# Two buffers for ScalarE's half of a decoding scratch, and one each for two small copies, in an attention and expert kernel

## The chip, the cores and the metric

The kernel runs on one core of a Trainium2 chip. The metric is device time in microseconds (us) of one launch. The kernel before ran three times: 1174.45, 1170.73 and 1174.22 us, median 1174.22 us.

## The reference

Eight batches of eight heads, 576 positions, head dimension 64, go through linear attention with 128 random features, and the result goes through a gated layer of 512 x 1536. All in float32:

```
proj = x @ w_phi                       # x is q or k
proj = proj - max(abs(proj), last axis)
phi(x) = concat(exp(proj), exp(-proj)) # 256 features
kv  = phi(k)^T v ;  z = sum over positions of phi(k)
attn = (phi(q) kv) / (phi(q) z + 1e-6)
X = attn as 4608 tokens x 512
out = ((X @ w_a) * (X @ w_b)) @ w_out
```

The weights w_a, w_b and w_out arrive in 64-bit form and have to be decoded on the chip: of each number the high and the low 32-bit word are read, and two float32 halves are made of them that TensorE multiplies by one after the other ("hi" and "lo").

## The kernel before, in words

A *pair* is two heads of one batch; there are 32. For each pair the kernel projects q and k, forms the features, multiplies, and divides; a pair takes four *turns* of a plan that is written out by hand (`attention_steps`). Beside the attention runs the first pass of the gated layer over the first 6 of 12 slices of the 1536 columns (`moe_block`), and after both a second pass over the other slices, with Strassen-like sums (`winograd`, from about 800 us on).

The weights of the first pass, 18 *units* (6 slices of each of w_a, w_b, w_out), are decoded during the attention by `load_weights`, in four steps a unit. The plan lets 0.8 steps go per turn from turn 5 on and 2.2 per turn from turn 40 on. A unit's life, all on tiles of 128 x 512:

1. ScalarE (L427, `Prelu`) turns the high words of the raw tile into `g`. It is queued behind the last exponential of the latest projection. Right behind it ScalarE's queue issues the transfer of the next unit's raw tile (L402); there are two raw tiles.
2. VectorE (L430) shifts `g` into `s`; (L432) masks `g`.
3. ScalarE (L435) casts `s` to the high half that TensorE uses.
4. VectorE (L437) multiplies the low words into `g` (last reader of the raw tile), (L438) takes the high half from `s`, and (L440) adds `s` and `g` to the low half.

`g` and `s` are the two halves of one tile `w` of 128 x 1024. It has one buffer in pool `a1`; up to turn 28 the units take it in turn from `a1` and from the pool `early`, so that two are in use there.

Two more tiles matter. `dn` (L299, L300) is the copy of a pair's row sums that ScalarE takes out of PSUM; SyncE (SP) stores it to HBM (L312, `den`), loads it back in another shape (L315), VectorE takes the reciprocal (L317), and it goes out (L319, `rec`) and is read back spread over the partitions (L323, `rb`), to be multiplied in (L326). `rk` (L159) holds the last 64 positions of k for two pairs. Both have two buffers.

What sets the order: TensorE's products in the attention are chained in the order in which the program writes them. ScalarE, VectorE and SP take their instructions strictly in the order of their queues; that order is made at build time by a planner, which walks the program with its own costs and puts an instruction into its engine's queue when its inputs, and the buffer that it writes, are free by these costs. So a change of buffers can change the order of the queues. [...]

PSUM results of the projection go through `p` copies: L201 copies the first half of q's projection, L213 the second; TensorE can write the second half of a pair's q (`pq`) only when L201 has emptied its buffer.

Of the kernel before, what the change touches and what calls it, by code (L numbers as in the profile page):

```python
# [9 lines left out]
F32 = mybir.dt.float32  # L10
# [8 lines left out]
P = 128  # L19
# [25 lines left out]
def tile_kernel(ctx, tc, qP, km, kr, vm, vr, w_phi, eye, w_a, w_b, w_out, out):  # L45
# [17 lines left out]
    DM, NT = out.shape  # L63
    DF = w_a.shape[0]
    NFULL = S // P
    HALF = S // 2
# [37 lines left out]
    def mm(out, w, x, start=True, stop=True):  # L104
        issue = lambda: nc.tensor.matmul(out, w, x, start=start, stop=stop, skip_group_check=True)  # L105
        return pe(issue) if alone else issue()
# [8 lines left out]
    def bank(tag, name):  # L115
        if "ps" in alone:
            return alone["ps"].tile([P, 3, P], F32, tag=tag, name=name)
        if tag == "kv":
            return alone["att"].tile([P, 3, P], F32, tag="kv", bufs=1, name=name)
        if tag == "pt":  # L120
            return alone["att"].tile([P, 2, 512], F32, tag="att", name=name)[:, 0, : 3 * P].rearrange("p (s f) -> p s f", s=3)
        return pools_moe[0].tile([P, 3, P], F32, tag="moe", name=name)
# [29 lines left out]
    def load_kq(b, pr, a1, a2, consts, st):  # L152
        u = f"{b}_{pr}"
        k32 = a2.tile([P, NFULL * P], F32, tag="k32", name=f"k32_{u}")
        loads.append(nc.sync.dma_start(k32, km[b, pr]))
        q32 = a2.tile([P, S], F32, tag="q32", name=f"q32_{u}")
        loads.append(nc.sync.dma_start(q32, qP[b, pr]))
        if pr % 2 == 0:
            rk = a2.tile([P, P], F32, tag="rk", name=f"rk_{u}")  # L159
            loads.append(nc.sync.dma_start(rk, kr[b, pr // 2]))  # L160
            st["rk", b, pr // 2] = rk
        st["k", b, pr], st["q", b, pr] = k32, q32
# [128 lines left out]
    def den_products(b, pr, a1, a2, consts, st):  # L291
        u = f"{b}_{pr}"
        kvh, eq = st["kvh", b, pr], st["eq", b, pr]
        pd = bank("pt" if "ps" in alone else "pd", f"pd_{u}").rearrange("p s f -> p (s f)")
        for s in range(2):
            for j in range(2):
                for t in range(2):
                    mm(pd[strips[2 * j + t], :HALF], kvh[:, 2, strips[2 * j + s]], eq[:, j, s, times[t]], start=(s == 0), stop=(s == 1))
        dn = st["dn", b, pr] = a2.tile([P, HALF], F32, tag="dn", name=f"dn_{u}")  # L299
        nc.scalar.activation(dn, pd[:, :HALF], AF.Identity, bias=consts[3])  # L300

    def behind(what, issue):
# [28 lines left out]
    def attention_steps(pools, consts, st):  # L331
# [11 lines left out]
        for i in range(B * NPAIR):  # L343
            b, pr = divmod(i, NPAIR)
            t0 = TURNS * i
            args = (b, pr, *pools, consts, st)
            at = SPREAD if i < ALONE else PACKED
            if i == ALONE - 1:
                at = dict(SPREAD, turned_kv=8, num_products=8, den_products=8)
            elif i == ALONE:  # L350
                at = dict(PACKED, kv_products=4, z_products=4, kv_out=4)
            units = ((project, 0), (q_features, TURNS), (turned_kv, 0), (summed, 0), (kv_products, 0), (num_products, 0), (z_products, 0), (kv_out, 0))
            units += ((den_products, 0), (load_kq, -5), (load_v, -2 if i else 0))
            for order, (f, t) in enumerate(units):
                if f is not summed or i >= SUM_FROM:
                    plan(order, once(f, *args), [t0 + at.get(f.__name__, t)])
            rec_turns = REC_TURNS0 if b < B - 1 else REC_TURNS
            done = t0 + at["den_products"]
            plan(10, reciprocals(b, pr, *pools, st), [done + t for t in rec_turns])
            if b == 0:  # L360
                plan(11, x_first, [done + rec_turns[-1] + t for t in X_TURNS])
            if pr == NPAIR - 1:
                plan(12, b, [done + rec_turns[-1]])
# [41 lines left out]
    def raw_tiles(units, stage):  # L405

        for f, nm in units:
            yield load_raw(0, f, nm, stage)

    def load_weights(units, a1):  # L410

        def stage(kind, shape, dt, name):
            return a1.tile(shape, dt, tag="raw", bufs=2, name=name)

        tiles = raw_tiles(units, stage)
        raws = deque([next(tiles)])
        yield
        for f, nm in units:
            raw = raws.popleft()
            u = f"0_{f}_{nm}"  # L420
            low, high = raw[:, :, 0], raw[:, :, 1]
            place = alone["early"] if alone["turn"] < TURNS * ALONE - 8 and len(weights) % 2 else a1
            w = place.tile([P, 2 * DM], F32, tag="w", name=f"w_{u}")
            g, s = w[:, :DM], w[:, DM:]
            gb, sb = g.bitcast(U32), s.bitcast(U32)
            with tc.issue_after(acts[-1].ins):
                prelu = nc.scalar.activation(g, high.bitcast(F32), AF.Prelu, scale=2.0**-112, alpha=2.0**32)  # L427
            with tc.issue_after(prelu.ins):
                raws.extend(itertools.islice(tiles, 1))
            nc.vector.tensor_scalar(sb, gb, 3, None, op0=ALU.logical_shift_left)  # L430
            yield
            nc.vector.tensor_scalar(gb, sb, 0xFF800000, None, op0=ALU.bitwise_and)  # L432
            t = wpool.tile([P, 2, DM], F32R, tag=f"w_{f}_{nm}", name=f"w_{u}")
            hi, lo = t[:, 0], t[:, 1]
            nc.scalar.copy(hi, s)  # L435
            yield
            nc.vector.scalar_tensor_tensor(g, low, 2.0**-52, g, op0=ALU.mult, op1=ALU.mult)  # L437
            nc.vector.tensor_tensor(s, s, hi, op=ALU.subtract)  # L438
            yield
            nc.vector.tensor_tensor(lo, s, g, op=ALU.add)  # L440
            weights[0, f, nm] = (hi, lo)
            yield
# [443 lines left out]
    with ExitStack() as c:  # L886
# [5 lines left out]
        work, tasks, due, coded, st = deque(), {}, 0.0, 0.0, {}  # L892
        units = [(f, nm) for f in range(NFS[0]) for nm in "ab"] + [(f, "o") for f in range(NFS[0])]
        decode_steps = placed(load_weights(units, pools[0]))
        for turn, ready in attention_steps(pools, consts, st):
            if ready is not None:
# [155 lines left out]
```

## Time and profile before

| | |
|---|---|
| three runs, median | 1174.22 us |
| the profiled execution | 1174.8 us |
| its span, first to last instruction | 1172.9 us |
| busy TensorE matmul / weight load | 97% / 88% |
| busy VectorE / ScalarE / GpSimd | 63% / 48% / 12% |
| mean granted TensorE clock | 0.994 |

The profile gives each instruction's start and duration in microseconds from the span's start, by engine: PE is TensorE, PEld its weight load, DVE VectorE, ACT ScalarE, SP SyncE; a q behind the name (SPq, ACTq) is the engine's queue, which issues transfers. Releasers of waits are inferred from semaphores. [...]

### The profile page before, as it was taken

Reading aid. Unit: us, or ns where it says so; the run is one execution under the profiler, and the core shown is the slowest. Engines: PE = TensorE matmul, PEld = TensorE weight load, DVE = VectorE, ACT = ScalarE, POOL = GpSimd, SP = SyncE. Lnnn points to the kernel's source line nnn. Section 1 sums busy time; section 2 is a strip of 40 time slices with the busy share of each in tenths; the row PEclk is TensorE's granted clock in tenths of the full one; section 3 lists DMA queues with packets and bytes.
Section 4 is the critical chain, followed back from the end, with each engine's and each line's share of the span. In section 5 each row is a group of like instructions: output and inputs, shape, how many; then the busy total and the mean of one; then the engine's idle time right before and its main releaser. Section 6 shows DMA issues by size and latency. Waiting matters only on the chain.

```text
span 1172.9 us, 20997 instructions
## 1 busy us (share of the span) xinstructions
PE 1143.1 (97%) x8198; PEld 1029.1 (88%) x8198; DVE 739.6 (63%) x1359; ACT 560.8 (48%) x1050; POOL 140.1 (12%) x69
## 2 busy tenths in 40 slices
PE   8998988999999899999999999999999999999998
PEld 6666776888788688889999999999999999999998
DVE  6886777545454454542225668958677695958675
ACT  6885665545454454552224445535344353425342
POOL 4442321212121121210000000000000000000000
PEclk9999989999999899999999999999999999999999
DMA  5566644324242232314103664458695867768582
GB/s 194 174 208 198 183 159 135 112 83 132 63 138 73 82 116 77 111 52 131 54 28 110 223 234 179 154 181 283 192 317 174 273 217 224 262 193 300 172 262 82
DMA packets 103076, 191.76 MB, mean 163 GB/s; under 512 B 19520, under 2 KB 54720, under 8 KB 102976
## 3 DMA queue, kind: packets, MB, share of 16 engines
q1 hardware_dynamic: 100080, 180.84, 48.0%
q10 hardware_dynamic: 2896, 9.57, 2.5%
q8 instruction: 65, 1.06, 0.4%
q14 instruction: 35, 0.29, 0.1%
HBM read 150.75 MB, written 39.62 MB: 162 GB/s over the span
## 4 chain that ended last, share of the span: by engine, by line
PE 81%; DVE 8%; DMA 6%; ACT 3%; issue 1%; SPq 0%; DVEq 0%; ACTq 0%
PE pa L105 13%; PE po L105 13%; PE pb L105 12%; PE po L782 10%; PE pa L671 9%; PE pb L671 8%; PE kv L105 6%; PE pn L105 4%; PE pq L105 2%; PE pd L105 2%; DMA rb<-rec 2%; DMA x<-xnorm 2%; DMA rec<-r 2%; PE pk L105 1%; DVE top L683 1%
## 5 line engine op out<-in xcount | busy, mean ns | idle before, releaser
L218 POOL PARTITION_ALL_REDUCE mb<-p x64 | 139.8, 2228 | 369.4 <-ACT p L213 363.1
L105 PE MATMUL pa<-xh,w_a 128*128 128x384 f32 x576 | 162.6, 344 | 0.0
L105 PE MATMUL pb<-xh,w_b 128*128 128x384 f32 x576 | 158.4, 336 | 0.0
L105 PE MATMUL po<-hh,w_o 128*128 128x384 f32 x576 | 153.2, 340 | 0.9 <-ACT hh L145 0.9
L105 PEld LDWEIGHTS pa<-xh,w_a 128*128 128x128 f32 x576 | 106.0, 190 | 6.8 <-issue 4.1
L105 PEld LDWEIGHTS po<-hh,w_o 128*128 128x128 f32 x576 | 104.5, 188 | 6.9 <-issue 3.4
L105 PEld LDWEIGHTS pb<-xh,w_b 128*128 128x128 f32 x576 | 105.1, 188 | 0.0
L560 DVE TENSOR_TENSOR h<-pb,h 128x384 f32<-128x384 f32 x72 | 39.9, 554 | 97.8 <-PE pb L105 95.5
L105 PE MATMUL po<-hl,w_o 128*128 128x384 f32 x288 | 96.8, 337 | 2.0 <-DVE hl L146 2.0
L105 PE MATMUL pa<-xl,w_a 128*128 128x384 f32 x288 | 97.3, 338 | 0.0
L105 PE MATMUL pb<-xl,w_b 128*128 128x384 f32 x288 | 96.8, 336 | 0.0
L180 DVE TENSOR_REDUCE m<-pk 128x8 f32<-128x1024 f32 x32 | 39.1, 1222 | 90.9 <-PE pk L105 90.8
L782 PE MATMUL po<-hh_s,own_o 128*128 128x384 f32 x288 | 80.1, 336 | 0.8 <-ACT u L770 0.7
L145 ACT CAST hh<-h 128x384 fp32r<-128x384 f32 x72 | 36.9, 512 | 80.3 <-DVE h L560 79.8
L105 PE MATMUL pn<-eq,kvh 128*64 128x288 f32 x512 | 68.3, 409 | 3.0 <-DVE kvh L276 2.9
L105 PE MATMUL kv<-e,v 128*64 128x256 f32 x512 | 64.1, 393 | 2.4 <-ACT e L184 2.3
L105 PEld LDWEIGHTS pn<-eq,kvh 128*64 128x64 f32 x512 | 37.6, 138 | 27.6 <-issue 3.1
L591 ACT COPY o<-po 128x384 f32<-128x384 f32 x48 | 22.6, 477 | 81.1 <-PE po L105 71.6
L559 ACT COPY h<-pa 128x384 f32<-128x384 f32 x72 | 34.3, 477 | 53.9 <-PE pa L105 51.9
L782 PE MATMUL po<-hh_w,own_o 128*128 128x384 f32 x216 | 58.8, 334 | 0.0
L105 PE MATMUL pq<-q,w 64*128 64x288 f32 x256 | 48.9, 452 | 9.8 <-ACT p L201 7.9
L105 PEld LDWEIGHTS po<-hl,w_o 128*128 128x128 f32 x288 | 54.2, 188 | 2.3 <-DVE hl L146 2.2
(257 smaller groups left out, 2619.5 us busy)
## 6 DMA issues: line engine op xcount, KB each, us to landing
back_s<-kept_s SPq DMA_DIRECT2D x71, 512.0 KB
back_w<-kept_w SPq DMA_DIRECT2D x52, 512.0 KB
q<-in_qP SPq DMA_DIRECT2D x32, 288.0 KB
rb<-rec SPq DMA_DIRECT2D x64, 144.0 KB
xnorm<-x SPq DMA_DIRECT2D x32, 288.0 KB
part<-o SPq DMA_DIRECT2D x48, 192.0 KB
o<-part SPq DMA_DIRECT2D x24, 384.0 KB
out_x<-o SPq DMA_DIRECT2D x48, 192.0 KB
```

Source lines behind the costliest of these rows:

```text
L105: issue = lambda: nc.tensor.matmul(out, w, x, start=start, stop=stop, skip_group_check=True)
L145: (eng_hi.copy if eng_hi is nc.scalar else eng_hi.tensor_copy)(hi, src)
L180: nc.vector.tensor_reduce(out=m, in_=p, op=ALU.max, axis=AX.X, apply_absolute_value=True)
L218: nc.gpsimd.partition_all_reduce(mb, p32[:, j], P, bass_isa.ReduceOp.absmax)
L559: nc.scalar.copy(h32, pab["a"])
L560: nc.vector.tensor_tensor(h32, pab["b"], h32, op=ALU.mult)
L591: passed.append(nc.scalar.copy(o, acc))
L671: in_turn(lambda: nc.tensor.matmul(acc[to][i], w_, x_, skip_group_check=True, **at), True)
L683: nc.vector.tensor_tensor(to[:, i], acc[k][i], to[:, i], op=ALU.add)
L782: in_turn(lambda: nc.tensor.matmul(acc[m, to], w_, h_, skip_group_check=True, **f), False)
```

## The change

The scratch tile `w` is split into its halves. `g`, which ScalarE writes first, is now a tile of its own with two buffers, always in `a1`. `s`, which VectorE writes, has one buffer, and alternates between `early` and `a1` as `w` did. `rk` and `dn` go from two buffers to one. No instruction is added, removed or resized; the engines and operands are the same. Per partition `a1` gains 2048 bytes and `a2` gives up 512 and 1152.

```
-            rk = a2.tile([P, P], F32, tag="rk", name=f"rk_{u}")
+            rk = a2.tile([P, P], F32, tag="rk", bufs=1, name=f"rk_{u}")
...
-        dn = st["dn", b, pr] = a2.tile([P, HALF], F32, tag="dn", name=f"dn_{u}")
+        dn = st["dn", b, pr] = a2.tile([P, HALF], F32, tag="dn", bufs=1, name=f"dn_{u}")
...
             low, high = raw[:, :, 0], raw[:, :, 1]
+            g = a1.tile([P, DM], F32, tag="wg", bufs=2, name=f"w_{u}_g")
             place = alone["early"] if alone["turn"] < TURNS * ALONE - 8 and len(weights) % 2 else a1
-            w = place.tile([P, 2 * DM], F32, tag="w", name=f"w_{u}")
-            g, s = w[:, :DM], w[:, DM:]
+            s = place.tile([P, DM], F32, tag="ws", name=f"w_{u}_s")
             gb, sb = g.bitcast(U32), s.bitcast(U32)
```

## Rows read from the trace of the kernel before

**Rows 1.** Busy time by stretch: TensorE, weight load, VectorE, ScalarE, GpSimd; clock; DMA.
```profile
30.00:220.00 190.00, 175.72 (x1940) 128.06 (x1937) 142.73 (x225) 130.08 (x202) 61.68 (x29) 0.98 0.56 174
220.00:1172.90 952.90, 942.34 (x5982) 882.40 (x5981) 577.03 (x1108) 410.42 (x820) 64.32 (x30) 1.00 0.50 160
```

**Rows 2.** Who waited for line L440, whole span: total us, times.
```profile
  ACT w_o L427: 7.5, 5
  ACT w_a L427: 4.1, 2
```

**Rows 3.** TensorE's waits, 30 to 220 us: total, times, longest.
```profile
PE pq L105 <- ACT p L201: 6.9, 3, 3.8
```

**Rows 4.** ScalarE near 148 us, in order of time: start, us, instruction [idle before].
```profile
148.28 0.66 ACT L427 ACTIVATE w_o<-raw_o 128x512 f32<-128x512 f32 x1 [2.25 <-DVE w_b L440]
...
149.44 0.62 ACT L435 CAST w_o<-w_o 128x512 fp32r<-128x512 f32 x1
```

**Rows 5.** VectorE in the same stretch.
```profile
143.75 0.76 DVE L326 TENSOR_TENSOR x<-x,rb 128x576 f32<-128x576 f32 x1 [4.00 <-DMA rb<-rec]
...
148.97 0.43 DVE L430 TENSOR_SCALAR w_o<-w_o 128x512 uint32<-128x512 uint32 x1 [0.73 <-ACT w_o L427]
```

**Rows 6.** TensorE's three products that wait for L201.
```profile
118.28 0.76 PE L105 MATMUL pq<-q,w 64*128 64x288 f32 x4 [0.21 <-ACT p L201]
...
151.04 1.33 PE L105 MATMUL pq<-q,w 64*128 64x288 f32 x4 [3.79 <-ACT p L201]
...
187.23 0.76 PE L105 MATMUL pq<-q,w 64*128 64x288 f32 x4 [2.89 <-ACT p L201]
```

**Rows 7.** The chain of waits, 152 and 158 us: start, us, piece.
```profile
152.37 3.70 PE pa L105 x12
...
158.48 2.08 PE pa L105 x12
```

**Rows 8.** Busy time by stretch around the first wait, columns as in rows 1.
```profile
148.00:149.00 1.00, 0.00 (x0) 0.00 (x0) 0.27 (x2) 0.72 (x2) 0.00 (x0) 0.80 0.32 94
149.00:155.00 6.00, 3.96 (x12) 3.21 (x13) 5.90 (x10) 4.90 (x8) 1.77 (x1) 0.50 0.58 183
```

**Rows 9.** ScalarE before the second wait.
```profile
184.87 0.66 ACT L427 ACTIVATE w_o<-raw_o 128x512 f32<-128x512 f32 x1 [1.87 <-DVE w_o L440]
```

**Rows 10.** VectorE before the second wait.
```profile
185.56 0.43 DVE L430 TENSOR_SCALAR w_o<-w_o 128x512 uint32<-128x512 uint32 x1 [0.72 <-ACT w_o L427]
```

**Rows 11.** SP's queue, stores of row sums and the loads behind them.
```profile
71.76 0.32 SPq L315 DMA_DIRECT2D r<-den  x1
...
111.28 1.96 SPq L508 DMA_DIRECT2D x<-xnorm  x4
113.33 0.52 SPq L312 DMA_DIRECT2D den<-dn  x1
117.08 0.31 SPq L315 DMA_DIRECT2D r<-den  x1
...
150.48 0.52 SPq L312 DMA_DIRECT2D den<-dn  x1
152.11 0.32 SPq L315 DMA_DIRECT2D r<-den  x1
```

**Rows 12.** ScalarE near 73, 115 and 169 us.
```profile
73.13 0.50 ACT L300 ACTIVATE dn<-pd,eps 128x288 f32<-128x288 f32 x1 [0.44 <-PE pd L105]
...
113.80 0.62 ACT L435 CAST w_a<-w_a 128x512 fp32r<-128x512 f32 x1 [6.13 <-DMA rb<-rec]
...
115.22 0.52 ACT L300 ACTIVATE dn<-pd,eps 128x288 f32<-128x288 f32 x1
115.62 0.49 ACT L559 COPY h<-pa 128x384 f32<-128x384 f32 x1
...
169.16 0.50 ACT L300 ACTIVATE dn<-pd,eps 128x288 f32<-128x288 f32 x1 [0.49 <-PE pd L105]
```

**Rows 13.** VectorE's product that follows that copy.
```profile
116.58 0.56 DVE L560 TENSOR_TENSOR h<-pb,h 128x384 f32<-128x384 f32 x1 [1.44 <-PE pb L105]
```
## The prediction

> **What bounds the kernel now.** I read the busy time by stretch first. TensorE is the bound: from 220 us to the end it is busy 942.34 of 952.90 us [rows 1], and of the changed tiles only `dn` and `rk` are used there (the last unit's shift is at 185.56 us [rows 10]). Between 30 and 220 us, where nearly all of the decoding lies, TensorE is busy 175.72 of 190 us, so 14.28 us of idle time is about all that the scratch can give back; clock apart, no better order in that stretch saves more.
>
> Second, the waits. The wait that the change aims at is L427 on L440: ScalarE may not write `g` of the next unit before VectorE has read the last unit's. It stands there seven times, 7.5 and 4.1 us, together 11.6 us [rows 2]. All seven come after 106 us. Up to turn 28 two scratch tiles alternate already, so the early units have nothing to win.
>
> Third, what TensorE waits for. Of its 14.28 us, 6.9 us in three waits are for L201, the copy that frees the projection's buffer [rows 3]: 3.79 us at 151.04, 2.89 us at 187.23, and 0.21 us at 118.28 [rows 6]. Only in front of the first two does an L427 wait stand in ScalarE's queue, of 2.25 and 1.87 us [rows 4, 9]. The other five, 7.5 us, hold up nothing that TensorE was waiting for: costed at nothing, their cover being the products already queued on TensorE.
>
> **Part one: two buffers for `g`.** What is late next when the L427 wait goes? Behind it in ScalarE's queue, ahead of L201, stands the cast L435, and that needs the shift L430 of the same unit. The shift writes `s`, which still has one buffer, and it is VectorE's own next decoding step after L440. So the cast cannot move ahead of L440; it only gains what VectorE idled between L440 and L430 while L427 ran: 0.73 us at 148.97 [rows 5] and 0.72 us at 185.56 [rows 10]. The rest of the 2.25 and 1.87 us turns into a wait of L435 on L430.
>
> At 151 us even the 0.73 us counts by half. [...] At 187 us the clock did not fall, and the gain is the whole 0.72 us. Part one: 0.37 + 0.72 = 1.09 us gained. Its bounds: nothing, if the planner leaves L427 where it is; and both waits, 3.79 + 2.89 us, with the lower clock's cost: pq took 1.33 us instead of 0.76 and twelve products 3.70 us instead of 2.08 [rows 6, 7], 2.19 us. That makes 8.87 us.
>
> L427 also pulls its raw transfer L402 along, on the same queue. The raw tile is free once L437 of the unit before last has run, two VectorE instructions before L440, so an early L427 can leave L402 waiting at the head of ScalarE's queue for a short while; I take nothing, with the bound under the second rival.
>
> **Part two: one buffer for `dn`.** It adds a wait: ScalarE may not write a pair's row sums before SP has stored the last pair's. Landing of the store is when the load behind it, L315, goes out. At 71.76 us it goes 1.37 us before the next `dn` at 73.13; later the distance is long: load at 152.11, next `dn` at 169.16. Once it is late: a store is issued at 113.33 and the load follows at 117.08, while the next `dn` is written at 115.22 [rows 11, 12]. There ScalarE will wait 1.86 us. Behind it stand the copy L559, ending at 115.62 + 0.49 = 116.11, the multiply on VectorE that started at 116.58 because TensorE's pb was late [rows 12, 13], the cast of its result, and L201. The slack is 0.47 us; 1.86 - 0.47 = 1.39 us reach TensorE at 118.28, where it is already waiting, by 0.21 us [rows 6]. From below the price is nothing, if the store is issued earlier in SP's queue; from above it is the whole 1.86 us. I take 1.39 us, since neither SP's wait for the reciprocals nor the loads ahead of the store are touched by the change.
>
> Why did that store take 3.75 us, where the one at 150.48 landed within 1.63 us [rows 11]? Four loads of x stand right ahead of it. [...]
>
> **Part three: one buffer for `rk`.** It is loaded with the k and q of the same pair, whose two buffers come free by the projection of two pairs before, the same that frees `rk`. It adds no later condition than its neighbours' by more than the few products behind them, and it is needed five turns later. Nothing; if that cover went, the price would be some 0.3 us of SP's queue, the length of one issue [rows 11].
>
> **Sum.** -0.37 - 0.72 + 1.39 = +0.30 us: 1175.1 us against the profiled execution's own 1174.8, which lies 0.6 us above the median of 1174.22. Against the median: 1174.5 us.
>
> **The rivals.** *Both stalls go.* The planner makes the queues anew. With `g` free it can put L427 right behind the exponentials, and the casts behind L201, so that neither 3.79 nor 2.89 us remains and the clock stays up: -8.87 us, and 1174.2 - 8.9 = 1165.3 us if `dn` costs nothing. For it: ScalarE is busy only 130 of 190 us [rows 1]. Against it: the cast's place in the queue is set by when the shift runs, and at 148 us VectorE was late for a reason that stays, 4.00 us of waiting for `rb` [rows 5]. Half of it would be 4.4 us, 1169.8 us.
>
> *ScalarE's queue stands behind a transfer.* The trace has one such case: it did nothing for 6.13 us up to 113.80, until a transfer of `rb` had landed [rows 12], as the raw transfer ahead of the cast shared its completion semaphore. It was cheap, since TensorE had 24 products of pa and pb, 2 x 2.08 = 4.2 us, to go on with by rows 7. Before 112 us there are no such products. If the raw transfers, now issued earlier, or a `dn` write come to stand so in a pair between 60 and 110 us, the price is 6.13 less the 1.39 already counted, plus 2.19 for a fall of the clock: +6.9 us, 1174.5 + 6.9 = 1181.4 us. It decides once a store of row sums lands 1.37 us later against the next `dn` than at 71.76. For it: that margin is small. Against it: of the stores shown, only the one behind four loads was late.
>
> *The change does nothing at all*, neither the gain nor the wait of `dn`: 1174.2 us; it counts with the forecast.
>
> **How the numbers follow.** About 0.3%, 3.5 us, is what a measurement of this kernel can tell from no change. The forecast and the case of nothing have 0.37 together. The first rival, from half of it on, has 0.37: 14 us of idle time lie open to a new order. The second has 0.26. The forecast's own range is 1171 to 1178 us; with the rivals' full prices at both ends it is 1165 to 1181 us. Since both signs hold most of the chance I keep all of it.
>
> **What would show it.** Right: L427 no longer waits for L440, L435 waits for L430 in its place; the waits of TensorE near 151 and 187 us are still there, 0.7 us shorter; the low clock after the first stays; ScalarE waits for a store before the `dn` near 115 us. Wrong: no TensorE wait over 2 us between 140 and 190 us, and the clock at 1.00 there (first rival), or a new ScalarE wait of over 3 us on a transfer with TensorE idle behind it (second). A difference after 220 us would mean that the new order of the queues matters more than the buffers.

## The result, and the profile after

The changed kernel took 1179.74 us, median of six runs (1177.29 to 1183.32). The kernel before, run beside it, took 1173.96 us, median of six. The ratio is 1.0054, 95% interval 1.0034 to 1.0073, so it is slower by 5.8 us. The forecast was 1174.5 us with a range of 1165 to 1181 us: the time lies in the range, near its slow end, and not at the likeliest case.

| | before | after |
|---|---|---|
| median | 1173.96 us | 1179.74 us |
| the profiled execution | 1174.8 us | 1177.29 us |
| its span | 1172.9 us | 1175.5 us |
| mean granted clock, profiled execution | 0.994 | 0.995 |
| mean granted clock over runs, those of the experiments too | 0.9952 (32 runs) | 0.9917 (15 runs) |

The profiled execution of after is the quickest of its six and is only 2.5 us longer than the profiled one of before. Its granted clock is no lower, while the last line shows a lower one on the mean; I come back to it. Nor do the 2.5 us all come from the decoding. Matched by the copies L289, after is 1.81 us late at 197 us, only 0.37 us late at 403 us, behind a stretch in which the clock was lower before (0.72 on the mean of 390 to 400 us, 0.83 after), and 2.6 us late at the end, behind 2.4 us of waits for `back_w` and `back_s` past 790 us that the profile of before does not have.

The stretches first, as in [rows 1]; columns as there:

```profile
30.00:220.00 190.00, 173.73 (x1928) 126.46 (x1926) 140.63 (x224) 128.87 (x200) 61.27 (x28) 0.98 0.57 174
220.00:1175.50 955.50, 943.08 (x5992) 883.11 (x5990) 578.84 (x1109) 412.08 (x821) 64.85 (x30) 1.00 0.49 160
```

TensorE's idle time in the decoding stretch went from 14.28 to 16.27 us: it stands still for 2 us more where the change was to give something back. Its products are the same and come in the same order, so what it waited for can be laid side by side. TensorE's waits from 30 to 220 us, after (total us, times, longest), and the one line of before that the forecast had not looked at:

```profile
PE pq L105 <- ACT p L201: 6.8, 3, 4.4
PE pt L274 <- ACT dn L300: 3.6, 2, 3.0
```
```profile
PE pt L274 <- ACT dn L300: 1.5, 1, 1.5
```

The waits for L201 are as long as before [rows 3] and a wait for `dn` has doubled. ScalarE's own waits in the same stretch tell why (after):

```profile
ACT w_o L435 <- DVE w_o_s L430: 6.7, 4, 2.0
ACT w_a L435 <- DVE w_a_s L430: 6.3, 3, 3.0
ACT w_o_g L427 <- DMA raw_o<-in_w_out: 3.5, 2, 2.1
...
ACT w_a_g L427 <- DMA raw_a<-in_w_a: 2.2, 2, 1.8
```

None of the waits of L427 for L440 [rows 2] is left. In their place L435 waits for L430, and L427 waits for its own raw transfer, which it never did in the profile of before.

**The first place, 107 us.** ScalarE in order of time, after; then the same work before:

```profile
102.21 0.34 ACTq L402 DMA_DIRECT2D raw_a<-in_w_a  x1
...
105.65 0.66 ACT L427 ACTIVATE w_a_g<-raw_a 128x512 f32<-128x512 f32 x1 [1.76 <-DMA raw_a<-in_w_a]
...
106.73 0.47 ACT L268 COPY back<-kv 128x384 f32<-128x384 f32 x1
107.10 0.51 ACT L300 ACTIVATE dn<-pd,eps 128x288 f32<-128x288 f32 x1
...
107.66 0.55 PE L274 MATMUL pt<-ident,back 128*128 128x128 f32 x3 [2.99 <-ACT dn L300]
```
```profile
104.59 0.49 ACT L300 ACTIVATE dn<-pd,eps 128x288 f32<-128x288 f32 x1
106.98 0.69 ACT L427 ACTIVATE w_a<-raw_a 128x512 f32<-128x512 f32 x1 [1.90 <-DVE w_b L440]
...
105.14 0.55 PE L274 MATMUL pt<-ident,back 128*128 128x128 f32 x3 [1.51 <-ACT dn L300]
```

Before, this L427 stood behind `dn`, and its wait for L440 came after TensorE had been let go. With a second `g` free, the planner puts it ahead of `dn`. Its transfer was issued at 102.21 us; ScalarE stands at the head of its queue until the data are there, `back` and `dn` behind it, and `pt` starts 1.48 us later against its neighbours.

**The second place, 153 us**, after:

```profile
147.05 0.34 ACTq L402 DMA_DIRECT2D raw_o<-in_w_out  x1
...
149.33 0.62 ACT L435 CAST w_o<-w_o_s 128x512 fp32r<-128x512 f32 x1 [0.83 <-DVE w_o_s L430]
152.07 0.66 ACT L427 ACTIVATE w_o_g<-raw_o 128x512 f32<-128x512 f32 x1 [2.12 <-DMA raw_o<-in_w_out]
...
152.63 0.49 ACT L300 ACTIVATE dn<-pd,eps 128x288 f32<-128x288 f32 x1
153.02 0.63 ACT L201 COPY p<-pq 128x576 f32<-128x576 f32 x1
...
153.70 1.33 PE L105 MATMUL pq<-q,w 64*128 64x288 f32 x4 [4.36 <-ACT p L201]
```

In [rows 4] one L427 stood in front of L201, for 2.25 us, because of L440. That unit's L427 is now early (143.54 us), and the next unit's has taken its place, 2.12 us for a transfer that could only go out at 147.05 us. The wait of TensorE is 4.36 us instead of 3.79.

**The third place, 189 us**, went as forecast; ScalarE, VectorE, TensorE, after:

```profile
187.82 0.62 ACT L435 CAST w_o<-w_o_s 128x512 fp32r<-128x512 f32 x1 [1.95 <-DVE w_o_s L430]
188.35 0.63 ACT L201 COPY p<-pq 128x576 f32<-128x576 f32 x1
...
187.36 0.43 DVE L430 TENSOR_SCALAR w_o_s<-w_o_g 128x512 uint32<-128x512 uint32 x1
...
189.03 0.76 PE L105 MATMUL pq<-q,w 64*128 64x288 f32 x4 [2.20 <-ACT p L201]
```

2.20 us instead of 2.89 [rows 6]: VectorE no longer idles 0.72 us ahead of L430 [rows 10], and the cast waits for L430 instead of L427 for L440.

### The profile page after: what moved, and what is told of

Its sections match the earlier page's. It is cut to its first block, busy times and chain, and to the rows that moved or that the text cites. A ratio compares the mean times of both kernels' runs of the same rounds, so it can differ in the third digit from the quotient of the medians.

```text
span 1175.5 us, 20999 instructions
## 1 busy us (share of the span) xinstructions
PE 1141.3 (97%) x8198; PEld 1028.0 (87%) x8198; DVE 739.4 (63%) x1359; ACT 561.3 (48%) x1050; POOL 140.3 (12%) x69
## 4 chain that ended last, share of the span: by engine, by line
PE 83%; DVE 7%; DMA 6%; ACT 3%; issue 1%; SPq 0%; ACTq 0%; DVEq 0%
PE pa L105 13%; PE po L105 12%; PE pb L105 12%; PE po L782 11%; PE pa L671 10%; PE pb L671 9%; PE kv L105 6%; PE pn L105 4%; PE pq L105 2%; PE pd L105 2%; DMA back_w<-kept_w 1%; PE pk L105 1%; DMA rb<-rec 1%; DMA rec<-r 1%; DMA x<-xnorm 1%
## 5 line engine op out<-in xcount | busy, mean ns | idle before, releaser
L218 POOL PARTITION_ALL_REDUCE mb<-p x64 | 140.0, 2232 | 369.6 <-ACT p L213 362.9
L559 ACT COPY h<-pa 128x384 f32<-128x384 f32 x72 | 34.4, 478 | 55.5 <-PE pa L105 53.6
```

The lines of the kernel that those rows point to most:

```text
L218: nc.gpsimd.partition_all_reduce(mb, p32[:, j], P, bass_isa.ReduceOp.absmax)
L559: nc.scalar.copy(h32, pab["a"])
```

## The experiments

All ratios are against the kernel before on the same chip. "Clock" is the mean over a kernel's runs of (1 - granted clock) x span, an estimate of what the lower clock cost. It is nearer to an upper bound: within one kernel, an execution with 1 us more of it took 0.4 to 1.0 us longer. The two last columns are TensorE's waits at the first and second place in the profiled execution.

| version | median, us | ratio, 95% interval | clock, us | pt near 107 | pq near 153 |
|---|---|---|---|---|---|
| before (first series) | 1173.62 | 1 | 5.6 | 1.51 | 3.79 |
| changed, again | 1180.03 | 1.0055 (1.0033 to 1.0077) | 9.8 | 2.59 | 3.41 |
| dn and rk alone | 1173.47 | 1.0005 (0.9988 to 1.0023) | 4.8 | 1.65 | 2.88 |
| one unit behind dn | 1175.43 | 1.0026 (1.0012 to 1.0041) | 7.5 | 1.27 | 4.37 |
| two units pinned | 1173.76 | 1.0010 (0.9990 to 1.0030) | 5.0 | 1.32 | 1.59 |
| two pinned, no lag | 1173.24 | 0.9982 (0.9964 to 1.0001) | 4.9 | 0.67 | 1.60 |
| two pinned, no lag, again | 1173.48 | 1.0002 (0.9985 to 1.0019) | 6.5 | 0.91 | 1.59 |
| two pinned and a cast | 1172.23 | 1.0000 (0.9983 to 1.0016) | 6.0 | 0.67 | 1.59 |
| before, same pins | 1173.99 | 1.0012 (0.9995 to 1.0029) | 6.8 | 1.40 | 3.13 |
| decoding in bursts | 1181.91 | 1.0056 (1.0034 to 1.0077) | 9.0 | 3.54 | 4.57 |
| changed, no transfers | 1171.43 | 0.9973 (0.9957 to 0.9989) | 5.8 | 1.87 | 2.07 |
| before, no transfers | 1169.95 | 0.9956 (0.9935 to 0.9976) | 3.9 | 1.27 | 2.01 |
| changed, raw on SP | 1175.78 | 1.0027 (1.0011 to 1.0043) | 8.0 | 4.34 | 4.62 |

The kernel before ran 32 times in the first series (the next four lines of the table), 29 times in the second (two pinned without lag, bursts, the two without transfers; 1174.95 us, clock 6.8 us), 29 times in the third (no lag again, the cast, the same pins; 1172.10 us, 5.5 us) and 17 times beside the last version (1172.09 us, 5.7 us), so versions of different series are compared by their ratios.

My theory: the planner's new order of ScalarE's queue costs the time, by an L427 that waits for its raw transfer ahead of `dn` and L201. The rivals: the single buffers of `dn` and `rk`, or chance.

**The changed kernel again** (no edit).

> The changed kernel once more. Theory (order of ScalarE's queue): 1.004 to 1.006 of the kernel before, and in the profile the same two places again, the product pt near 107.7 us waiting about 3.0 us for ScalarE's dn (before 1.5) and pq near 153.7 us waiting about 4.4 us for L201 (before 3.8), with L427 standing in front of both for its raw transfer. Rival (chance in the waits for transfers after 400 us and in falls of the clock): the two places come and go from profile to profile, and the difference between two profiles of this kernel is as large as the 2.5 us between it and the one before.

The ratio came out again. The profiled execution had L427 ahead of `dn` and of L201 again, waiting 0.66 and 1.39 us for its transfers, and TensorE waited at both places. One sign of the rival came too: this execution took 1174.43 us, the shortest of nine and 2.9 us below the first profiled one, and so no longer than the kernel before's. So no profile shows the whole loss; it stands on the medians. There is a third place in it. ScalarE and TensorE near 147 us:

```profile
145.82 0.34 ACTq L402 DMA_DIRECT2D raw_o<-in_w_out  x1
146.25 0.64 ACT L289 COPY x<-pn 128x576 f32<-128x576 f32 x1 [1.40 <-DVE w_b_g L437]
...
146.94 1.38 PE L105 MATMUL pk<-w,k 64*128 64x128 f32 x16 [2.68 <-ACT x L289]
```

L402, the transfer that an early L427 pulls along, stood at the head of the queue until L437 had freed the raw tile, and the copy L289 behind it let TensorE wait. In the first profile the same 1.40 us lay beside a late `pd`. The lower clock shows here: from 90 to 200 us it is 0.94 on the mean, against 0.97 in the first profile and before, and it falls near 190 us too (0.79 from 190 to 195 us, 1.00 in both others). Against my number for the second place, it was 3.41 us and not 4.4: TensorE had already lost time at 147 us.

**The small buffers alone.**

```
 rk = a2.tile([P, P], F32, tag="rk", bufs=1, ...)      # as in the change
 dn = ... a2.tile([P, HALF], F32, tag="dn", bufs=1, ...)
 w = place.tile([P, 2 * DM], F32, tag="w", ...)        # as before
```

> Only the edits of dn and rk, the decoding scratch as before. Theory (order of ScalarE's queue, made by the scratch): no difference, ratio 0.998 to 1.002, TensorE's waits at 107.7, 151 and 187 us as before (1.5, 3.8, 2.9 us); ScalarE waits about 1 us for a store ahead of the dn near 115 us and TensorE does not. Rival (the single dn buffer, or the loads of rk that go out later on SP's queue): 1.003 to 1.006, with the pt near 107.7 us waiting 3 us already here. By the working of the forecast, dn alone would cost 1.4 us: 1.001.

No difference: `dn` and `rk` are out. ScalarE's order up to 230 us is that of the kernel before, so it is the buffer of `g` that changes the order. The wait of `dn` is there, with a small price in this execution. ScalarE and TensorE:

```profile
116.30 0.50 ACT L300 ACTIVATE dn<-pd,eps 128x288 f32<-128x288 f32 x1 [1.53 <-DMA den<-dn]
...
118.89 0.76 PE L105 MATMUL pq<-q,w 64*128 64x288 f32 x4 [0.50 <-ACT p L201]
```

ScalarE waits 1.53 us for the store, TensorE 0.50 us instead of 0.21 [rows 6].

**One unit behind dn.**

```
-            with tc.issue_after(acts[-1].ins):
+            behind_dn = tc.issue_after(late[-1].ins) if (f, nm) == (4, "a") else nullcontext()
+            with tc.issue_after(acts[-1].ins), behind_dn:
                 prelu = ...                    # late: the dn copies (L300) so far
```

> The changed kernel with one instruction moved: the L427 of unit (4, a) goes into ScalarE's queue behind the dn near 107 us instead of three places ahead of it. Theory (queue order): the pt near 107.7 us waits 1.2 to 1.7 us instead of 3.0, and the time is 1 to 2 us below the changed kernel in the same call. Rival (the buffers of dn and rk, or chance): no difference from the changed kernel beyond 0.5 us, with the wait of pt staying near 3 us for another reason.

One instruction of ScalarE's queue is moved by three places, and 4.6 us of the 6.4 go by the medians (1180.03 to 1175.43), more than the 1 to 2 us that I expected; the intervals of the two ratios overlap, so the size is not well known. The added lines shift the numbers by one, so L427 is L428 here. ScalarE and TensorE:

```profile
106.14 0.49 ACT L300 ACTIVATE dn<-pd,eps 128x288 f32<-128x288 f32 x1
106.54 0.66 ACT L428 ACTIVATE w_a_g<-raw_a 128x512 f32<-128x512 f32 x1
...
106.69 0.55 PE L274 MATMUL pt<-ident,back 128*128 128x128 f32 x3 [1.27 <-ACT dn L300]
```

L427 no longer waits at all, since its transfer has landed by then. By the means 3.9 us go, of which the clock is up to 2.3 (9.8 to 7.5, by the estimate above); the wait of `pt` is 1.3 to 1.7 us shorter.

**Two units pinned, and without the lag.** The second unit's L427 goes behind L201; for that its decoding begins one step later. In the version without lag it makes the step up by doing two in one.

```
+            if (f, nm) == (1, "o"):
+                yield
+            pin = {(4, "a"): late, (1, "o"): first}.get((f, nm))   # first: the L201 so far
...
             nc.scalar.copy(hi, s)
-            yield
+            if (f, nm) != (1, "o"):            # only in the version without lag
+                yield
```

> As the one-unit version, and the decoding of unit (1, o) begins one step later, with its L427 behind the L201 near 153 us instead of ahead of it; the units after it shift by one place. Theory (queue order): in addition the pq near 153.7 us waits 2 us or less instead of 4.4, and the clock falls there for a shorter time or not at all; 3 to 6 us below the changed kernel, so 0.999 to 1.002 of the kernel before. Rival (the raw transfer itself is late because the two raw tiles come free late, wherever L427 stands): the wait moves to the next projection or to the weights' first use, and the gain over the one-unit version is under 1 us.

> As the version with two units pinned, but unit (1, o) makes up its lost step by doing two in one, so that the last units are decoded as early as in the changed kernel. Theory (queue order): the pq near 153 us waits 1.6 us as in the version with two units pinned, and that version's new wait of 2.50 us, a product of po near 191 us for the last w_o, is gone: 1 to 2.5 us below it, 0.998 to 1.000 of the kernel before. Rival (the pin only moves the wait, since VectorE and the raw tiles set the pace of the last units): no difference from the version with two units pinned, and the wait near 191 us, or one as long between 170 and 200 us, is there again.

> The version with two units pinned and no lag once more, as a second sample of its time and a second profile. Theory: 0.997 to 1.000 of the kernel before, the wait of pq near 147 to 152 us at 1.6 us again. Rival (the first sample was a lucky one): 1.000 or above.

The place near 153 us in the version without lag, ScalarE and TensorE (L439 is the cast L435, and L444 the sum L440, in these versions):

```profile
145.71 0.50 ACT L300 ACTIVATE dn<-pd,eps 128x288 f32<-128x288 f32 x1
146.10 0.63 ACT L201 COPY p<-pq 128x576 f32<-128x576 f32 x1
...
146.78 0.76 PE L105 MATMUL pq<-q,w 64*128 64x288 f32 x4 [1.60 <-ACT p L201]
```

In all three runs pq waits 1.6 us. With both units out of the way the change is back at the time of the kernel before, and the clock's cost is about that of the kernel before in the same series (5.0 us beside 5.6, 4.9 beside 6.8, 6.5 beside 5.5). The version with lag had a new wait, as feared:

```profile
192.62 0.44 PE L105 MATMUL po<-hh,w_o 128*128 128x384 f32 x1 [2.50 <-DVE w_o L444]
```

It is not there without the lag. But the two samples without lag, 0.9982 and 1.0002, together show no gain over the kernel before: the second one also had the wait of L289 near 147 us (1.60 us).

**And a cast behind L201.** The edit is the same kind of pin on L435 of unit (3, o), which also goes into the unit's next step for it.

> As the version with two units pinned and no lag, and the cast L435 of unit (3, o) goes behind the L201 near 166 us instead of two places ahead of it. Theory (queue order): the pq there, which waited 1.76 us in that version, waits under 0.7 us: 0.5 to 1.5 us below it, 0.996 to 0.999 of the kernel before. Rival (VectorE's decoding steps set the pace of the last units): the cast comes later, L438 and L440 of that unit and the next one's shift with it, and the gain is given back near 182 us, where pq then waits 2.5 us or more instead of 1.67: no difference.

pq near 170 us did not wait at all, but neither did it in the second sample of the version without this edit, so the 1.76 us that I aimed at was one execution's. 1.0000: no difference can be told.

**The kernel before with the same pins.**

> The kernel before, one buffer for g and s together and two for dn and rk, with the same edits as the version with two units pinned and no lag; of these only the step of unit (1, o) changes a queue here, since L427 of unit (4, a) is behind dn already. Theory (one buffer makes L427 of unit (0, o) wait for L440 in front of L201 near 151 us, and no edit here touches that): no gain, 0.999 to 1.002 of the kernel before, with the wait of 3.8 us near 151 us still there; so the version with two units pinned owes what it gained to g's second buffer. Rival (it owes it to the later step of unit (1, o) alone): 0.997 to 0.999 here too, and pq near 151 us waits 1.6 us or less.

1.0012, and pq still waits 3.13 us, with L427 of unit (0, o) in front of L201 for 2.24 us. So the second buffer of `g` does shorten the second place to 1.6 us once the order is mended; it is only not enough to beat the kernel before.

**Decoding in bursts.**

```
-                coded += DECODE_ALONE if turn < begin else DECODE_BESIDE
+                coded += DECODE_ALONE if turn < begin else (2 * DECODE_BESIDE if turn % 4 < 2 else 0)
```

> The changed kernel with another plan from turn 40 on: 4.4 decoding steps in each of the two turns that begin with a projection, none in the two turns ahead of the next one (2.2 in each of the four before). Theory (queue order): no L427 or L435 of a late unit stands ahead of L201, so TensorE's waits for L201 near 153 and 189 us fall from 4.4 and 2.2 us to under 1 us each and the clock stays up there: 5 to 9 us below the changed kernel, 0.997 to 1.001 of the kernel before. Rival (VectorE is the tight engine right behind a projection): decoding steps there delay the reductions and kvh, TensorE waits for kvh or the features in their place, and the time is that of the changed kernel or above, 1.005 or more.

The time is that of the changed kernel, as the rival had it, but not for the rival's reason. The planner made the same order, with L427 ahead of `dn` and L201 (ScalarE):

```profile
154.50 0.66 ACT L427 ACTIVATE w_o_g<-raw_o 128x512 f32<-128x512 f32 x1 [2.33 <-DMA raw_o<-in_w_out]
...
155.06 0.49 ACT L300 ACTIVATE dn<-pd,eps 128x288 f32<-128x288 f32 x1
155.45 0.64 ACT L201 COPY p<-pq 128x576 f32<-128x576 f32 x1
```

When a step is written down in the plan does not decide its place in the queue; the planner's idea of when its inputs are ready does. The experiment tells nothing between the two.

**Without the transfers**, of the changed kernel and of the kernel before.

```
-        for f, nm in units:
-            yield load_raw(0, f, nm, stage)
+        two = [load_raw(0, *units[i], stage) for i in range(2)]
+        for i in range(len(units)):
+            yield two[i % 2]
```

> The changed kernel without the raw transfers from the third unit on: the first two units' raw tiles are decoded again and again, so 16 of 18 transfers are left out and the weights are wrong; ScalarE's queue keeps its order otherwise. Theory (an L427 that stands ahead of dn and L201 costs only what it waits for its transfer): L427 waits for no transfer, pt near 107.7 us waits about 1.5 us and pq near 153.7 us 2 to 3 us, and the time is 4 to 7 us below the changed kernel, 0.998 to 1.001 of the kernel before. Rival (the place in the queue costs, with or without a transfer, or VectorE is late): under 2 us below the changed kernel.

> The kernel before with the same 16 raw transfers left out. It says what the missing transfers are worth by themselves, and whether two buffers for g gain anything once the raw tile is no limit. Theory (in the kernel before L427 waits for L440, not for its transfer): 0 to 2 us below the kernel before; the waits of L427 for L440 remain, 10 to 12 us in all, and the other kernel without transfers is equal to this one or up to 1.1 us faster (the forecast's gain). Rival (both waits for L201 go with g's second buffer, once the transfer is out of the way): the other one is faster by 4 to 9 us.

In the kernel before, ScalarE's order stays as it is. In the changed kernel it does not quite, against what I had written: four of the L427, those at both places among them, move up past one or two more copies or casts (L427 is L428 here, and L440 is L441). ScalarE and TensorE of the changed kernel without transfers:

```profile
102.46 0.69 ACT L428 ACTIVATE w_a_g<-raw_a 128x512 f32<-128x512 f32 x1
...
104.47 0.51 ACT L300 ACTIVATE dn<-pd,eps 128x288 f32<-128x288 f32 x1
...
105.03 0.55 PE L274 MATMUL pt<-ident,back 128*128 128x128 f32 x3 [1.87 <-ACT dn L300]
...
145.68 0.68 ACT L428 ACTIVATE w_o_g<-raw_b 128x512 f32<-128x512 f32 x1 [2.24 <-DVE w_b L441]
```

Ahead of `dn` L427 now costs its own 0.7 us and no wait, and `pt` waits 1.87 us, where it waited 2.99. So the place alone is cheap there, and the wait for the transfer is what is dear. Ahead of L201 it is not so simple: L427 runs up to the sum L440 of the unit before last and waits 2.24 us for it, as the kernel before did [rows 4], though pq waits only 2.07 us. The changed kernel gains 9.6 us without transfers (1.0055 to 0.9973 of 1173.6 us), the kernel before 5.2 us (0.0044 of 1174.95): 4.4 us of the loss go with them, give or take some 4 us by the three intervals. I had expected 0 to 2 us for the kernel before. What changed most there is VectorE's wait for `rb`, 30 to 220 us, before and without transfers:

```profile
DVE x L326 <- DMA rb<-rec: 11.8, 6, 4.0
```
```profile
DVE x L326 <- DMA rb<-rec: 1.1, 1, 1.1
```

So the waits for `rb` go with the 16 raw transfers: near 143 us there were 4.00 us of them [rows 5], and 1.14 us without the transfers. And the forecast's first rival is refuted: with no transfer in the way, two buffers for `g` are not faster than one (0.9973 against 0.9956, intervals overlapping).

**Raw transfers on SP's queue.**

```
-        (nc.sync if p else nc.scalar).dma_start(raw...)
+        nc.sync.dma_start(raw...)
```

> The changed kernel with the 18 raw transfers (L402) issued on SP's queue instead of ScalarE's; ScalarE's own work keeps its order but for one copy. It separates the two waits that an early L427 brings: L427 itself for its landed transfer, and the issue of the next transfer, L402, for the raw tile that L437 frees, which held up L289 behind it by 1.40 us near 147 us. Theory (both count): L289 no longer waits for L437, pk near 147 us waits under 0.8 us, while L427 still waits for its transfer ahead of dn near 107 us and of L201 near 153 us: 1 to 4 us below the changed kernel, 1.001 to 1.005 of the kernel before. Rival one (only L427's own wait counts): no difference, 1.005 to 1.006. Rival two (SP's queue stands behind the raw tile instead, so den, r and rb come late, and VectorE's L326 waits over 5 us for rb): 1.007 or more.

L289 near 147 us waits only 0.15 us, for its own product, and pk not at all; L427 still waits ahead of `dn` and L201, and longer (ScalarE):

```profile
104.35 0.67 ACT L427 ACTIVATE w_a_g<-raw_a 128x512 f32<-128x512 f32 x1 [3.14 <-DMA raw_a<-in_w_a]
...
146.92 0.64 ACT L289 COPY x<-pn 128x576 f32<-128x576 f32 x1 [0.15 <-PE pn L105]
...
153.64 0.66 ACT L427 ACTIVATE w_o_g<-raw_o 128x512 f32<-128x512 f32 x1 [3.02 <-DMA raw_o<-in_w_out]
```

The ratio is 1.0027, half of the loss, in the middle of what the theory said, and below what rival one said: the wait of L427 alone is not all. That the gain is L402's is not shown. The waits for `rb`, of which rival two expected more, fell from 11.8 to 7.2 us, which may be part of it, while SP's queue itself stood at L402 for L437 three times, 8.1 us in all. And this profiled execution, at 1177.22 us one of the longer ones of the version, has longer waits of TensorE at both places than the changed kernel (4.34 and 4.62 us), so it does not show where the gain lies. The order is not quite the same either: L427 is one copy further up near 104 and near 130 us.

## Why the prediction was right or wrong

The likeliest case, 1174.5 us, was 5.2 us too low, and its own range ended at 1178 us. That the time lies in the full range is owed to the second rival's price at its slow end, and that price was made of the wrong row (below): in part luck.

**What bounds the kernel: right, as far as the profiles show.** Matched by the copies L289 near 91 and 197 us, the changed kernel falls back 2.2 us in its first profile and 2.8 us in its second, with TensorE's waits between. No profile shows where the rest of the 5.8 us lies.

**Part one, the wait that takes the place: right in the mechanism, at one place of two.** L435 waits for L430, and the stall near 187 us shrank by 0.69 us, where 0.72 was forecast. Near 151 us it was to shrink by 0.7 and grew by 0.57, because another unit's L427 had moved into the gap. The 0.37 us that the sum took for this place is half of 0.73 us, an estimate of mine from the clock of 0.50 in [rows 8] and from pq's 1.33 us there instead of 0.76 [rows 6]; no run shows such a term, only the wait that grew.

**The step that failed** is the one behind part one: "an early L427 can leave L402 waiting at the head of ScalarE's queue for a short while; I take nothing, with the bound under the second rival". I saw that L427 pulls L402 along and asked only about the issue, not about L427's own input. Three things were wrong with that nothing:

- L427 itself waits for its transfer, 1.76 and 2.12 us in the first profile (0.66 and 1.39 in the second), ahead of `dn` and of L201. Two `g` buffers made the two raw tiles the next limit: a raw tile comes free at L437 of the unit before last, and L427 ran 5.0 us after its transfer's issue (147.05 to 152.07). In the kernel before, the wait for L440 had hidden that, and near 107 us it had kept L427 behind `dn`.
- L402 holds up L289 by 1.40 us, which TensorE feels in some executions (2.68 us near 147 us in the second profile) and not in others.
- The clock. In the sum I counted it only where it fell already. Over the runs its cost, by the estimate above, rose from 5.6 us to 9.7 us, by up to 4.2 of the 6.4 us between the means (1179.6 us of 15 runs and 1173.2 of 32). It was 4.9 to 6.5 us when both units were pinned, which points at the new waits; that they do it is not shown fall by fall. The second profile shows one new fall, near 190 us.

**Part two, `dn`: a term mis-sized.** Forecast 1.39 us. ScalarE did wait, 0.82 us in the first profile (1.86 forecast), but the copy L559 behind it had to wait for TensorE's pa anyway, and the store landed sooner. In the other profiles with one buffer the wait was up to 3.9 us (2.22 in the second profile, where TensorE's pq still waited 0.21 us); TensorE felt 0.4 us of it at most (0.60 instead of 0.21 us, two units pinned). ScalarE, then SP's queue, after:

```profile
115.05 0.50 ACT L300 ACTIVATE dn<-pd,eps 128x288 f32<-128x288 f32 x1 [0.82 <-DMA den<-dn]
116.97 0.48 ACT L559 COPY h<-pa 128x384 f32<-128x384 f32 x1 [1.42 <-PE pa L105]
...
110.89 2.31 SPq L508 DMA_DIRECT2D x<-xnorm  x4
113.26 0.52 SPq L312 DMA_DIRECT2D den<-dn  x1
...
115.03 0.32 SPq L315 DMA_DIRECT2D r<-den  x1
```

The four loads of x are still ahead of the store, and the load behind it goes out after 1.77 us, not after 3.75 [rows 11]; behind the same four loads it was 2.37 us in the second profile and 3.32 us with the small buffers alone. So the four loads ahead of the store do not by themselves account for the 3.75 us. What made the store late is open.

**Part three, `rk`: right**, nothing, by the version with the small buffers alone.

**The rivals.** The first (both stalls go) was refuted by the profiles, 4.36 and 2.20 us; the pair without transfers shows no gain of two buffers either. The second came nearest: a raw transfer issued earlier, ScalarE's queue standing behind it, between 60 and 110 us, and a fall of the clock, 1181.4 us. Its sign and its place near 107 us were right. Its price was made of the wrong row: the wait is not the 6.13 us of a cast L435 behind an `rb` [rows 12], of which the first profile has nothing and the second 3.26 us, behind a `rec`; it is one for the data, 0.3 to 3.4 us, four times in each profile. Its deciding condition, a late store of row sums, had nothing to do with it. With the trace of the kernel before I could have given it more: L427 at 106.98 stood behind `dn`; its transfer went out at 102.33 us, and near 551 us the trace has such a transfer with ScalarE waiting for it, 3.4 us from issue (L402, 550.97) to use (L389, 554.41). By that (an estimate) the data landed near 105.7 us, so that any place ahead of the `dn` at 104.59 meant a wait. In the changed kernel it took 3.4 us too (102.21 to 105.65).

**What stays open.** In which executions the clock falls at which place; where the part of the loss lies that neither profile shows; and the waits for `back_w` and `back_s` after 790 us, from nothing to 2.6 us in all, whatever the version. I take them for chance, since the small buffers alone, no slower than the kernel before, had 2.6 us of them; this is not shown.

## What to carry to other kernels

A second buffer took away one condition here, and L427 then ran up to its next one (1.76 and 2.12 us). Before you count the gain, ask what that next condition is (here the landing of a transfer that waits on the other double buffer) and which critical instruction it will then stand in front of. A wait that sits behind the critical instruction may cost nothing, as L427's 1.90 us behind `dn` near 107 us in the kernel before, and it may be what keeps the order right. The same second buffer, with two instructions pinned behind their critical neighbours, cost nothing that can be told. And price a new wait of TensorE at more than its length: here, by the estimate above, the lower clock may have cost up to 4.2 of 6.4 us.

## What the runs showed of the hardware that I had not expected

**Operations of VectorE with two operands in SBUF took longer when they started just after one of GpSimd.** In the version with one unit behind `dn` TensorE waits 2.57 us near 90 us, where it waited 1.08 us in the kernel before, although nothing was changed there. The version with two units pinned has the same 2.57 us. VectorE in the changed kernel, then in that version:

```profile
87.84 0.63 DVE L440 TENSOR_TENSOR w_b<-w_b_s,w_b_g 128x512 fp32r<-128x512 f32 x1
```
```profile
87.83 1.72 DVE L441 TENSOR_TENSOR w_b<-w_b_s,w_b_g 128x512 fp32r<-128x512 f32 x1
89.47 0.54 DVE L276 COPY kvh<-pt 128x384 f32<-128x384 f32 x1
...
90.17 3.85 PE L105 MATMUL pn<-eq,kvh 128*64 128x288 f32 x16 [2.57 <-DVE kvh L276]
```

The same sum took 0.63 and 1.72 us. The second of GpSimd's two reductions (L218) there started at 88.02 us in the first, 0.18 us after it, and at 87.63 us in the second, 0.20 us ahead of it. The trace of the kernel before has six such cases between 20 and 200 us: VectorE operations with two operands in SBUF (L219, L326, L437, L438, L440) that start 0.1 to 0.5 us after a GpSimd instruction take 0.93 to 1.13 us longer, those at 0.9 to 1.05 us take 0.12 to 0.56 us longer, and those from 1.3 us on nothing, though GpSimd is shown as running 2.1 to 2.5 us. L181, with one operand in PSUM, took the same 1.22 us (0.42 us for its small form) at every distance from 0.07 to 1.9 us. The mask L432, with one operand in SBUF, does not fit: it took 0.6 us longer at 0.54 us and again at 1.71 us. The spans of GpSimd in a profile are rough, so its real end may be earlier. What makes the operations longer is not shown. Here a reduction that started 0.39 us earlier went with a sum that took 1.09 us longer, and the products behind it ran at a low clock as well (0.66 on the mean of 90 to 95 us, against 1.00): matched by the first product behind pn, some 3 us were lost there.

**Raw transfers that no instruction was seen to wait for cost 5 us in the kernel before**: leaving out 16 of them took VectorE's waits for `rb` from 11.8 to 1.1 us and the kernel before from 1174.95 to 1169.95 us.
